# A third slot of tokens from the counts of the first eight groups, and work of the first words and the first group moved to VectorE

## The chip, the cores and the metric

The kernel runs on one core of one Trainium2 chip. The metric is device time in microseconds (us): the median of three runs before the change is 834.08 us, from 831.96 to 835.83.

## The reference

Three layers follow one another on 4 x 576 = 2304 tokens of 512 features:

```python
# attention by random features, 4 x 8 heads, 576 tokens, 64 dims, 128 features
h = q_s @ omega.T - sum(q_s**2)/2;  q_p = exp(h - max(h)) / sqrt(128)   # k_p alike
num = q_p @ (k_p.T @ v);  den = q_p . sum(k_p) + 1e-6
x = num / den
# dense feed-forward net, 512 -> 2048 -> 512
h = x @ w_in;  g = h * clip(h + 3, 0, 6) / 6;  x = g @ w_out
# mixture of 8 experts, each token goes to the one with the largest logit
logits = x @ w_gate + modality_bias[modality_id]
e = argmax(logits);  gate = softmax(logits)[e]
out[token] = gate * (relu(x @ w1[e]) @ w2[e])      # 512 -> 1024 -> 512
```

All is float32. The inputs give very uneven experts: two of the eight take 1161 and 1143 of the 2304 tokens, the others none.

## The kernel before

**Stages.** The tokens are cut into nine groups of G = 256. First the keys and values of all heads are summed up (`k_unit`). Then each group of queries goes through `q_unit` (exponentials, denominators, division, product with the summed keys and values), one unit for each pair of heads, and gives the group's rows x. Each group then runs 16 steps of the dense net; a step is one block of 128 hidden features, with a first product h (12 matmuls) and a second product y (6 matmuls). Each float32 operand is split in a high and a low part of a type that TensorE multiplies at full rate (`split`, L398), and a product is the sum of three; the low part of a step's activations is called gl, the high part gh. Group 0 works with whole float32 weights instead.

**Words.** The dense weights come as pairs of 32-bit words (the low and the high word of a wider number). `convert` (L509) makes a float32 from each pair: ScalarE takes the sign and the exponent's lead from a half word, VectorE ors the sign in, ScalarE scales the high word, and VectorE shifts and ors the rest. The first NW0 = 8 tiles of words are converted while group 0's queries are worked on; group 0's division is done head by head, on whichever of VectorE, ScalarE and GpSimd the order's cost model finds free.

**Routing.** When a group's y is done, `route` (L876) gives each token its expert, its position in a list sorted by expert, and scatters token number and gate to the table `order` in memory (DMAs on GpSimd's queue, 18 in all).

**Slots.** The expert layer works in slots of 256 tokens of one expert, numbered in the order in which they are worked on. A slot has eight steps of the same two products. Ten slots are laid out statically: the first NE from the counts of the first eight groups, by `first_slots` (L1196), which takes NE times the largest remaining count; the rest by `slot_table` (L1227) from the counts of all nine groups. The last static slot runs only its first 128 rows statically; further slots would run under a condition, and with these inputs there are none. The last group's scatter waits until the tokens of the first NE slots were loaded (the gate in `route` on `st["toks"]`), since those slots read `order` without it.

For each slot `slot_fetch` (L1125) loads the slot's token numbers from `order` (tile `tok`, on SP's queue), clips them to row numbers (`src`, on VectorE), and gathers the rows of the dense net's output (`xr<-yrows,src`, two DMAs of 128 rows on GpSimd's queue). `slot_rows` (L1146) transposes them on TensorE (eight matmuls with the identity, in the banks kp and kv) and splits them. `slot_weights` (L1091) loads each slot's 16 weight tiles (`wraw`) and splits them, on ScalarE and VectorE (`w<-wraw`). `slot_out` (L1175) scales y by the gate and scatters it to the output.

**Order.** Nothing of this is written down in a fixed order. The class `Issue` keeps all streams as tasks; its `run` (L255) asks a cost model which task could start first on which engine, takes by priority among those close together, and so writes each engine's instruction list, once, when the program is built. On the chip each engine works its list strictly in order. `t_fetch` (L1163) and `t_rows` (L1168), the streams of fetches and transposes, have the priority TOKENS (L32). A fetch may be issued once the slot before the last has its rows, and a slot's transposes once `x_free` (L1381) holds, that is when all first products of the slot before the last have been issued.

Of the kernel before, what the change touches and what calls it, by code (L numbers as in the profile page):

```python
# [18 lines left out]
P = 128  # L19
# [15 lines left out]
def f32(ap):  # L35
    return ap.bitcast(F32)
# [265 lines left out]
def favor_ffn_top1_moe_kernel(  # L302
# [28 lines left out]
    NT = N // P  # L331
    NO = E * N + G
    PAD = 1 << 20
    NE = 2
    NS_MIN = NG + 1 - NE
    NS_MAX = (N - G - (N - 2 * G) // E + E * (G - 1)) // G
    NKV = 6
    NW = 2 * KF
    NB = 4
# [128 lines left out]
    def conv():  # L468
# [40 lines left out]
        def convert(j):  # L509
            c, which = j // 2, j % 2  # L510
            yield Gate(cond=lambda: j in staged)
            t = yield from place(c, which)
            w = staged.pop(j)
            lo_w, hi_w = w[:, :, 0], w[:, :, 1]


            ti = t.bitcast(I32)
            half = w.rearrange("p n w -> p (n w)").bitcast(U16).rearrange("p (n w) -> p n w", w=4)
            yield from op(
                "A", "activation", out=ti, in_=half[:, :, 1], func=AF.Copy, scale=2.0 ** -13, bias=2.0 ** -14 - 0.5  # L520
            )

            yield from op(
                "V", "scalar_tensor_tensor", out=ti, in0=hi_w, scalar=-(1 << 31), in1=ti, op0=ALU.bitwise_and, op1=ALU.bitwise_or
            )
            yield from ts(f32(hi_w), f32(hi_w), 2.0 ** -112, ALU.mult, e="A")
            yield from op(
                "V", "scalar_tensor_tensor", out=ti, in0=hi_w, scalar=3, in1=ti,
                op0=ALU.logical_shift_left, op1=ALU.bitwise_or,
            )  # L530
            done.add(j)
            w_full[which, c] = t
# [271 lines left out]
    def q_unit(k, g, pr, tags):  # L804

        rr = list(runs(g * G, G))
        if g:
            yield from l_qh.take()
        qp, den = k.kp[0], k.den
        if k.two:  # L810
            yield from stack(qhl, k.qraw)
            mx = q.tile(rt, [P, 4], F32, "mx", 8)
            yield from project(qhl, P, GT, tags[0], qp, mx)
            pv = qp
        else:
            mx = None
            raw = k.qraw
            if g:
                raw, hi, lo = raw[:, 0], qhl[:, 0], qhl[:, 1]
                yield from split(hi, lo, raw)  # L820
            ps = bank(tags[0], [P, GT, 2 * M])
            yield q.gate("PE", [hi, lo] if g else [raw, om_f], [ps])
            for t in range(GT):
                c = slice(t * P, (t + 1) * P)
                if g:
                    mm3(ps[:, t], (hi[:, c], lo[:, c]), (om2[:, 0, :], om2[:, 1, :]))
                else:
                    do("PE", "matmul", out=ps[:, t], lhsT=raw[:, c], rhs=om_f, start=True, stop=True)
            pv = ps.rearrange("p t (h m) -> p (t h) m", m=M)
        if g:  # L830
            l_qh.give()
        yield from phi(pv, P, 2 * GT, qp, mx)
        if not all((b, pr) in z_t for _, _, b, _ in rr):
            yield Gate(cond=lambda: all((b, pr) in z_t for _, _, b, _ in rr))

        for t in range(GT):
            for o, n, b, s in runs(g * G + t * P, P):
                for h in range(2):
                    i = 2 * t + h
                    yield from op(  # L840
                        "V", "scalar_tensor_tensor", out=junk[o:o + n, i * M:(i + 1) * M], in0=qp[o:o + n, i, :], scalar=1.0,
                        in1=z_t[b, pr][o:o + n, h, :], op0=ALU.mult, op1=ALU.mult, accum_out=den[o:o + n, i:i + 1],
                    )
        yield from ts(den, den, 1e-6 * M, ALU.add)
        yield from op("V", "reciprocal", out=den, in_=den)
        if k.two:
            yield from tt(qp, qp, den.unsqueeze(2).to_broadcast([P, 2 * GT, M]), ALU.mult)
        else:
            for i in range(2 * GT):
                yield from ts(qp[:, i], qp[:, i], den[:, i:i + 1], ALU.mult, e=("V", "A", "P"))  # L850
        ps = bank(tags[-1], [P, 2, G])
        yield q.gate("PE", [qp], [ps])
        transposes([(ps[:, h, t * P:(t + 1) * P], qp[:, 2 * t + h, :]) for h in range(2) for t in range(GT)])
        yield from op(("A", "V"), "tensor_copy", out=k.qe, in_=ps)
        ps = bank(tags[0], [P, G])
        yield q.gate("PE", [k.qe] + [kv_t[b, pr] for _, _, b, _ in rr], [ps])
        for o, n, b, s in rr:

            for h in range(2):
                c = slice(h * D, (h + 1) * D)  # L860
                do(
                    "PE", "matmul", out=ps[c, o:o + n], lhsT=kv_t[b, pr][:, c], rhs=k.qe[:, h, o:o + n],
                    start=True, stop=True, skip_group_check=True,
                )
            q_open.remove(b * NPR + pr)
        if g and not (st["setup"] and st["n_in"] >= (g - 1) * KF):
            yield Gate(cond=lambda: st["setup"] and st["n_in"] >= (g - 1) * KF)
        xt = q.tile(ff, [P, 2, G], F32R if g else F32, f"x{pr}", 2)
        if g:
            yield from split(xt[:, 0], xt[:, 1], ps)  # L870
        else:
            yield from op(("A", "V"), "tensor_copy", out=xt[:, 0], in_=ps)
        x_t[g, pr] = xt
# [248 lines left out]
            done[0] = j + 1  # L1122
            st["split"] += 1

    def slot_fetch(mo, s):  # L1125

        yield q.gate("S", [s.o])
        at_ = q.load(s.o, E * N)
        s.tok = q.tile(mo, [P, GT, 2], I32, "tok", 6)
        yield from op("S", "dma_start", out=s.tok, in_=order[bass.ds(at_, G), :].rearrange("(t p) w -> p t w", p=P))  # L1130
        st["toks"] += 1
        src = q.tile(mo, [P, GT], I32, "src", 2)
        n = N if s.i >= NE else N - G
        yield from ts(src, s.tok[:, :, 0], n - 1, ALU.min)
        rows = []
        for t in range(GT):
            xr = q.tile(mo, [P, DM], F32, f"xr{t}", 2)
            yield from op(
                "P", "indirect_dma_start", out=xr, out_offset=None, in_=yrows[0:n, :],
                in_offset=bass.IndirectOffsetOnAxis(ap=src[:, t:t + 1], axis=0),  # L1140
                bounds_check=n - 1, oob_is_err=False,
            )
            rows.append(xr)
        s.rows = rows
# [16 lines left out]
        s.x = x  # L1161

    def t_fetch(mo, ss):  # L1163
        for i, s in enumerate(ss):
            yield Gate(cond=lambda: s.o is not None and (i < 2 or len(ss[i - 2].x) == KD))
            yield from slot_fetch(mo, s)

    def t_rows(ss, free):  # L1168
# [234 lines left out]
        q.run()  # L1403

    def rest(s):
        yield from slot_fetch(mo, s)
        yield from slot_rows(s, ("kp", "kv"))
        ys = None
# [63 lines left out]
```

## Time and profile before

| what | value |
| --- | --- |
| median of three runs | 834.08 us (831.96 to 835.83) |
| the profiled execution's own time | 834.48 us |
| its span in the trace | 832.8 us |
| mean granted TensorE clock | 0.983 of full speed |
| chain that ended last | issue 36%, TensorE 33%, DMA 15%, VectorE 8%, ScalarE 4% |

In the page's 40 slices TensorE's busy share is 9 tenths or more in all but five: the first two, the last, the one from 562 us (8 tenths) and the one from 625 us (5 tenths), where the granted clock is at 7 tenths. VectorE is the next busiest, with 8 or 9 tenths in most slices of the first half. The DMA engines are nearly idle from 140 to 560 us, and at 8 or 9 tenths in most slices from 625 to 770 us, where the experts' weights are loaded. Such a page is read stage by stage: an engine's share of the whole span says little of any one stage, and an idle stretch of the engine that is busy nearly all the time is time that some wait has cost.

### The profile page before, as it was taken

How to read it: one execution, taken by the hardware profiler on the slowest of the kernel's cores; microseconds unless marked ns; L12 is line 12 of the kernel's file. 1: busy time of each engine (PE TensorE's matmuls, PEld its weight loads, DVE VectorE, ACT ScalarE, POOL GpSimd, SP SyncE). 2: the span in 40 equal slices, each digit the busy share in tenths (PEclk: the TensorE clock that was granted, in tenths of full speed). 3: DMA queues.
4: the chain of work that ended last, by engine and by line, in shares of the span. 5: the costliest groups of instructions: out<-in, count | busy, mean ns of one | idle time of the engine just before them, and what ended most of it. 6: DMA issues, size and time to landing. Idle time of an engine off the chain costs nothing.

```text
span 832.8 us, 16519 instructions
## 1 busy us (share of the span) xinstructions
PE 791.0 (95%) x5395; PEld 675.0 (81%) x5395; DVE 630.8 (76%) x2135; ACT 487.1 (58%) x1245; POOL 99.7 (12%) x114
## 2 busy tenths in 40 slices
PE   7799999999999999999999999998995999999994
PEld 5476668888888888888888888987884898999993
DVE  3889999888888868878788785667986777777610
ACT  3998786777757556555655453335445766555411
POOL 0132342000000000110000000002013122211000
PEclk9989999999999999999999999999997999999997
DMA  7717574222113022221120010009359899877300
GB/s 182 278 52 228 168 243 132 51 54 83 51 33 81 13 53 68 32 61 47 41 64 27 1 39 1 26 15 289 94 171 293 276 289 273 270 219 207 103 13 29
DMA packets 108767, 96.88 MB, mean 116 GB/s; under 512 B 14847, under 2 KB 90111, under 8 KB 108672
## 3 DMA queue, kind: packets, MB, share of 16 engines
q1 hardware_dynamic: 104976, 85.75, 35.8%
q0 software_dynamic: 3696, 9.98, 3.5%
q8 instruction: 45, 0.74, 0.4%
q14 instruction: 50, 0.41, 0.2%
HBM read 86.10 MB, written 9.87 MB: 115 GB/s over the span
## 4 chain that ended last, share of the span: by engine, by line
issue 36%; PE 33%; DMA 15%; DVE 8%; ACT 4%; POOL 1%; SPq 1%; POOLq 0%; DVEq 0%; ACTq 0%
PE h L223 14%; PE y L223 9%; DMA wraw<-in_w_dram 5%; DMA order<-og,pi 4%; DVE w L223 4%; PE qa L223 3%; PE qb L223 3%; ACT w L223 2%; PE kv L223 2%; PE kp L223 2%; DMA xr<-yrows,src 1%; DMA kraw<-in_kT_dram 1%; SPq L223 1%; POOL order L223 1%; DMA w<-in_v_dram 1%
## 5 line engine op out<-in xcount | busy, mean ns | idle before, releaser
L223 PE MATMUL h<-x,w 128*128 128x256 f32 x2616 | 367.6, 290 | 2.1 <-DVE gl L223 0.9
L223 PEld LDWEIGHTS h<-x,w 128*128 128x128 f32 x2616 | 343.0, 191 | 22.5 <-issue 3.8
L223 PE MATMUL y<-w,gh 128*128 128x512 f32 x640 | 205.2, 402 | 0.0
L223 PE MATMUL y<-w,gl 128*128 128x512 f32 x320 | 126.0, 394 | 0.0
L223 PEld LDWEIGHTS y<-w,gh 128*128 128x128 f32 x640 | 110.2, 190 | 18.2 <-issue 3.0
L223 DVE TENSOR_TENSOR w<-wraw,w 128x512 fp32r<-128x512 f32 x160 | 106.3, 687 | 20.3 <-ACT w L223 16.4
L223 ACT ACTIVATE w<-wraw 128x512 fp32r<-128x512 f32 x152 | 91.2, 627 | 29.1 <-DMA wraw<-in_w_dram 25.7
L223 ACT ACTIVATE r<-h,three 128x256 f32<-128x256 f32 x144 | 68.1, 473 | 62.5 <-PE h L223 52.4
L223 DVE SCALAR_TENSOR_TENSOR junk<-st,words 128x512 bf16<-128x512 f32 x144 | 98.8, 686 | 1.2
L223 ACT ACTIVATE gh<-r 128x256 fp32r<-128x256 f32 x126 | 52.5, 417 | 80.3 <-PE y L223 75.1
L223 DVE SCALAR_TENSOR_TENSOR r<-r,h 128x256 f32<-128x256 f32 x144 | 60.3, 419 | 28.2 <-ACT r L223 24.8
L223 DVE TENSOR_TENSOR gl<-r,gh 128x256 fp32r<-128x256 f32 x128 | 54.3, 424 | 34.4 <-ACT gh L223 22.0
L223 PEld LDWEIGHTS y<-w,gl 128*128 128x128 f32 x320 | 60.5, 189 | 14.3 <-DVE gl L223 0.3
L223 POOL DMA_INDIRECT order<-og,pi x18 | 19.1, 1064 | 406.9 <-DVE pi L223 261.4
L223 ACT ACTIVATE gh<-h 128x256 fp32r<-128x256 f32 x72 | 27.4, 380 | 60.1 <-PE qb L223 22.4
L223 DVE SCALAR_TENSOR_TENSOR gl<-h,gh 128x256 fp32r<-128x256 f32 x72 | 30.4, 422 | 31.9 <-ACT gh L223 29.1
L223 ACT ACTIVATE kp<-kp,mx 112x128 f32<-112x128 f32 (+1 forms) x120 | 38.8, 387 | 1.2 <-DVE mx L223 1.0
L223 POOL DMA_INDIRECT out_dram<-st,tok x19 | 19.8, 1040 | 162.5 <-ACT gh L223 77.7
L223 DVE SCALAR_TENSOR_TENSOR junk<-qp,zb 128x128 bf16<-128x128 f32 (+1 forms) x144 | 37.4, 286 | 1.4 <-ACT qp L223 0.2
L223 ACT ACTIVATE qp<-qp,mx 128x128 f32<-128x128 f32 x104 | 36.2, 393 | 0.0
L223 DVE SCALAR_TENSOR_TENSOR w<-words,w 128x512 int32<-128x512 int32 x44 | 31.7, 748 | 0.0
L223 PE MATMUL kp<-om,khl 128*112 128x256 f32 (+1 forms) x140 | 29.4, 307 | 1.5 <-DVE khl L223 1.0
(270 smaller groups left out, 1069.4 us busy)
## 6 DMA issues: line engine op xcount, KB each, us to landing
wraw<-in_w_dram SPq DMA_DIRECT2D x160, 256.0 KB
words<-in_w_in_dram SPq DMA_DIRECT2D x12, 512.0 KB
words<-in_w_out_dram SPq DMA_DIRECT2D x12, 512.0 KB
qraw<-in_qT_dram SPq DMA_DIRECT2D x36, 128.0 KB
yrows<-st SPq DMA_DIRECT2D x18, 256.0 KB
kraw<-in_kT_dram SPq DMA_DIRECT2D x40, 112.0 KB
vraw<-in_v_dram SPq DMA_DIRECT2D x24, 112.0 KB
w<-in_w_in_dram SPq DMA_DIRECT2D x4, 512.0 KB
```

Source lines behind the costliest of these rows:

```text
L223: return getattr(self.eng[e], m)(**kw)
```

## The change

Three edits, in four places of the code:

1. `NE` goes from 2 to 3, so `first_slots` picks three slots; `NS_MIN` falls from 8 to 7 with it, the static slots stay ten, and `NS_MAX`, the bound on slots of the table, falls from 15 to 14. The load of a slot's tokens is taken out of `slot_fetch` into `slot_tokens`, and `t_fetch` loads the tokens of all three first slots before the first slot's `src`. `src` gets three buffers instead of two.
2. For the first eight tiles of words, `convert` uses one scaling on ScalarE, one scaling on VectorE (which carries the sign) and two shift-and-or operations on VectorE, instead of the half-word operation and the scaling on ScalarE with two such operations on VectorE.
3. Group 0's division is one VectorE operation for a unit, not four small ones on three engines.

```diff
--- before.py
+++ after.py
@@ -331,9 +331,13 @@
     NT = N // P
     NO = E * N + G
     PAD = 1 << 20
-    NE = 2
+    NE = 3
     NS_MIN = NG + 1 - NE
-    NS_MAX = (N - G - (N - 2 * G) // E + E * (G - 1)) // G
+
+    taken_min = G
+    for _ in range(NE - 1):
+        taken_min += min(G, -(-(N - G - taken_min) // E))
+    NS_MAX = (N - taken_min + E * (G - 1)) // G
     NKV = 6
     NW = 2 * KF
     NB = 4
@@ -512,6 +516,18 @@
             t = yield from place(c, which)
             w = staged.pop(j)
             lo_w, hi_w = w[:, :, 0], w[:, :, 1]
+            if j < NW0:
+
+                ti = t.bitcast(I32)
+                yield from ts(f32(hi_w), f32(hi_w), 2.0 ** -112, ALU.mult, e="A")
+                yield from ts(t, f32(hi_w), 2.0 ** -126, ALU.mult)
+                for w_, n, f in ((lo_w, 29, ALU.logical_shift_right), (hi_w, 3, ALU.logical_shift_left)):
+                    yield from op(
+                        "V", "scalar_tensor_tensor", out=ti, in0=w_, scalar=n, in1=ti, op0=f, op1=ALU.bitwise_or
+                    )
+                done.add(j)
+                w_full[which, c] = t
+                return
 
 
             ti = t.bitcast(I32)
@@ -843,7 +859,7 @@
                     )
         yield from ts(den, den, 1e-6 * M, ALU.add)
         yield from op("V", "reciprocal", out=den, in_=den)
-        if k.two:
+        if k.two or not g:
             yield from tt(qp, qp, den.unsqueeze(2).to_broadcast([P, 2 * GT, M]), ALU.mult)
         else:
             for i in range(2 * GT):
@@ -1122,14 +1138,16 @@
             done[0] = j + 1
             st["split"] += 1
 
-    def slot_fetch(mo, s):
-
+    def slot_tokens(mo, s):
         yield q.gate("S", [s.o])
         at_ = q.load(s.o, E * N)
         s.tok = q.tile(mo, [P, GT, 2], I32, "tok", 6)
         yield from op("S", "dma_start", out=s.tok, in_=order[bass.ds(at_, G), :].rearrange("(t p) w -> p t w", p=P))
         st["toks"] += 1
-        src = q.tile(mo, [P, GT], I32, "src", 2)
+
+    def slot_fetch(mo, s):
+
+        src = q.tile(mo, [P, GT], I32, "src", NE)
         n = N if s.i >= NE else N - G
         yield from ts(src, s.tok[:, :, 0], n - 1, ALU.min)
         rows = []
@@ -1161,8 +1179,13 @@
         s.x = x
 
     def t_fetch(mo, ss):
+        for s in ss[:NE]:
+            yield Gate(cond=lambda: s.o is not None)
+            yield from slot_tokens(mo, s)
         for i, s in enumerate(ss):
             yield Gate(cond=lambda: s.o is not None and (i < 2 or len(ss[i - 2].x) == KD))
+            if i >= NE:
+                yield from slot_tokens(mo, s)
             yield from slot_fetch(mo, s)
 
     def t_rows(ss, free):
@@ -1403,6 +1426,7 @@
         q.run()
 
     def rest(s):
+        yield from slot_tokens(mo, s)
         yield from slot_fetch(mo, s)
         yield from slot_rows(s, ("kp", "kv"))
         ys = None
```

What the order makes of the first edit shows best on three engines' lists, behind the count of the first eight groups.

VectorE before: the small operations of `first_slots` (c, h, mx, eo, taken), slot 0's `src`, and the first split of an expert's weights (`w<-wraw,w`):

```order
L223 TENSOR_TENSOR h_7063<-h_7063 128x8
L223 TENSOR_TENSOR gl<-r,gh 128x256
L223 TENSOR_REDUCE mx_7062<-h_7063 128x1
L223 CAST eo<-mx_7062 128x1
L223 TENSOR_SCALAR mx_7062<-mx_7062 128x1
L223 TENSOR_SCALAR h_7063<-h_7063,mx_7062 128x8
L223 TENSOR_SCALAR src<-tok 128x2
L223 TENSOR_TENSOR taken<-taken,h_7063 128x8
L223 TENSOR_TENSOR c_7045<-c_7045,h_7063 128x8
L223 TENSOR_TENSOR w<-wraw,w 128x512
L223 SCALAR_TENSOR_TENSOR r<-r,h_7150 128x256
```

VectorE with the change, the same place; the second `src` is slot 1's:

```order
L223 TENSOR_SCALAR mx_7059<-mx_7059 128x1
L223 TENSOR_TENSOR gl<-r,gh 128x256
L223 TENSOR_SCALAR h_7060<-h_7060,mx_7059 128x8
L223 TENSOR_TENSOR w<-wraw,w 128x512
L223 TENSOR_TENSOR taken<-taken,h_7060 128x8
L223 TENSOR_TENSOR c_7043<-c_7043,h_7060 128x8
L223 TENSOR_TENSOR w<-wraw,w 128x512
L223 TENSOR_SCALAR src<-tok 128x2
L223 TENSOR_TENSOR w<-wraw,w 128x512
L223 TENSOR_SCALAR st<-y_6761 128x512
L223 TENSOR_TENSOR w<-wraw,w 128x512
L223 TENSOR_SCALAR src<-tok 128x2
```

Slot 0's `src` stood three rows ahead of the first weight split; it now stands behind the group's last difference (`gl<-r,gh`) and in the middle of the weight splits, six of which come ahead of it from there and the rows before.

TensorE before: slot 0's second four transposes (bank kv, rows `xr_7185` and `xr_7193`) end, its first two steps' products h follow, and slot 1's transposes (`xr_7315`, `xr_7321`) come behind them:

```order
L223 MATMUL kv<-ident,xr_7185 128x128
L223 MATMUL kv<-ident,xr_7193 128x128
L223 MATMUL h_7367<-x_7302,w 128x256 x3
L223 MATMUL h_7367<-x_7317,w 128x256 x3
L223 MATMUL h_7367<-x_7349,w 128x256 x3
L223 MATMUL h_7367<-x_7358,w 128x256 x3
L223 MATMUL h_7392<-x_7302,w 128x256 x3
L223 MATMUL h_7392<-x_7317,w 128x256 x3
L223 MATMUL h_7392<-x_7349,w 128x256 x3
L223 MATMUL h_7392<-x_7358,w 128x256 x3
L223 MATMUL kp<-ident,xr_7315 128x128
L223 MATMUL kp<-ident,xr_7321 128x128
```

TensorE with the change: slot 1's transposes (`xr_7329`, `xr_7339`) stand ahead of slot 0's first product:

```order
L223 MATMUL kv<-ident,xr_7306 128x128
L223 MATMUL kv<-ident,xr_7314 128x128
L223 MATMUL kv<-ident,xr_7306 128x128
L223 MATMUL kv<-ident,xr_7314 128x128
L223 MATMUL kp<-ident,xr_7329 128x128
L223 MATMUL kp<-ident,xr_7339 128x128
L223 MATMUL kp<-ident,xr_7329 128x128
L223 MATMUL kp<-ident,xr_7339 128x128
L223 MATMUL h_7417<-x_7356,w 128x256 x3
L223 MATMUL h_7417<-x_7378,w 128x256 x3
```

The first product of slot 0 so stands behind the gathers of both slots.

GpSimd's queue before, from the last scatters of the first eight groups (`order` x16) on; the gathers of slots 0 and 1, the output of slot 0 (`out_dram`) and the last group's scatter, and slot 2's gathers (`xr_8038`, `xr_8048`):

```order
L223 DMA order<-og,pi 18688x2 x16
L223 DMA xr_7185<-yrows,src 128x512
L223 DMA xr_7193<-yrows,src 128x512
L223 DMA xr_7315<-yrows,src 128x512
L223 DMA xr_7321<-yrows,src 128x512
L223 DMA out_dram<-st,tok 2304x512 x2
L223 DMA order<-og,pi 18688x2 x2
L223 DMA out_dram<-st,tok 2304x512
L223 DMA xr_8038<-yrows,src 128x512
L223 DMA xr_8048<-yrows,src 128x512
```

GpSimd's queue with the change; `xr_7414` and `xr_7477` are slot 2's rows:

```order
L223 DMA order<-og,pi 18688x2 x16
L223 DMA xr_7306<-yrows,src 128x512
L223 DMA xr_7314<-yrows,src 128x512
L223 DMA xr_7329<-yrows,src 128x512
L223 DMA xr_7339<-yrows,src 128x512
L223 DMA xr_7414<-yrows,src 128x512
L223 DMA xr_7477<-yrows,src 128x512
L223 DMA out_dram<-st,tok 2304x512 x2
L223 DMA order<-og,pi 18688x2 x2
L223 DMA out_dram<-st,tok 2304x512 x2
L223 DMA xr_8279<-yrows,src 128x512
L223 DMA xr_8286<-yrows,src 128x512
```

Slot 2's gathers moved from behind the last group's scatter to ahead of slot 0's output.

## Rows read from the trace of the kernel before

**Rows 1.** The page's first part: engine, busy us, share of the span, instructions.

```profile
PE 791.0 (95%) x5395; PEld 675.0 (81%) x5395; DVE 630.8 (76%) x2135; ACT 487.1 (58%) x1245; POOL 99.7 (12%) x114
```

**Rows 2.** TensorE's waits, 560 to 645 us: us, times, longest.

```profile
PE kp L223 <- DMA xr<-yrows,src: 10.9, 3, 8.0
```

**Rows 3.** Timeline, slot 1's end to slot 2: start, us, engine, operation [wait].

```profile
624.13 0.40 PE L223 MATMUL y<-w,gl 128*128 128x512 f32 x1
...
626.80 0.17 DVE L223 TENSOR_SCALAR src<-tok 128x2 int32<-128x2 int32 x1
...
627.75 1.38 POOL L223 DMA_INDIRECT xr<-yrows,src  x1 [1.20 <-issue]
...
629.43 1.01 POOL L223 DMA_INDIRECT xr<-yrows,src  x1 [0.31 <-issue]
...
632.50 0.45 PE L223 MATMUL kp<-ident,xr 128*128 128x128 f32 x1 [7.97 <-DMA xr<-yrows,src]
...
635.29 0.90 PE L223 MATMUL kp<-ident,xr 128*128 128x128 f32 x3 [2.34 <-DMA xr<-yrows,src]
...
636.70 6.29 PE L223 MATMUL h<-x,w 128*128 128x256 f32 x36
...
642.83 0.63 PE L223 MATMUL qa<-w,gh 128*128 128x512 f32 x2
```

**Rows 4.** Busy time by stretch, slot 2's start: engines, clock, DMA share.

```profile
632.50:637.00 4.50, 2.15 (x9) 1.81 (x9) 1.00 (x3) 0.38 (x1) 2.03 (x2) 0.50 0.99 301
```

**Rows 5.** Timeline from the count of eight groups to slot 0's first products.

```profile
554.06 0.18 PE L223 MATMUL kv<-acc,ones 128*128 128x8 bf16 x1
...
563.61 1.05 POOL L223 DMA_INDIRECT xr<-yrows,src  x1 [7.80 <-DMA wraw<-in_w_dram]
...
564.97 1.01 POOL L223 DMA_INDIRECT xr<-yrows,src  x1 [0.31 <-issue]
...
571.03 0.55 PE L223 MATMUL kp<-ident,xr 128*128 128x128 f32 x3 [0.56 <-DMA xr<-yrows,src]
...
573.23 1.53 POOL L223 DMA_INDIRECT xr<-yrows,src  x1 [7.25 <-DVE src L223]
...
575.76 0.60 PE L223 MATMUL kv<-ident,xr 128*128 128x128 f32 x4
...
576.11 1.10 PE L223 MATMUL h<-x,w 128*128 128x256 f32 x7
...
577.63 2.58 PE L223 MATMUL h<-x,w 128*128 128x256 f32 x15 [0.42 <-DVE x L223]
```

**Rows 6.** The chain that ended last: one first and one second product.

```profile
582.27 1.43 PE h L223 x12
...
715.60 1.39 PE y L223 x6
```

**Rows 7.** Costliest groups, VectorE: busy us, mean ns, idle before.

```profile
L223 DVE TENSOR_TENSOR w<-wraw,w 128x512 fp32r<-128x512 f32 x160 | 106.3, 687 | 20.3 <-ACT w L223 16.4 <-issue 0.5
...
L223 DVE TENSOR_TENSOR gl<-r,gh 128x256 fp32r<-128x256 f32 x128 | 54.3, 424 | 34.4 <-ACT gh L223 22.0 <-PE kp L223 7.7 <-PE qa L223 1.8
...
L223 DVE SCALAR_TENSOR_TENSOR w<-words,w 128x512 int32<-128x512 int32 x44 | 31.7, 748 | 0.0
...
L223 DVE TENSOR_TENSOR qp<-qp,den 128x512 f32<-128x512 f32 x26 | 17.9, 687 | 0.2
...
L223 DVE CAST w<-wraw 128x512 fp32r<-128x512 f32 x8 | 3.4, 426 | 1.6 <-DMA wraw<-in_w_dram 1.6
```

**Rows 8.** Timeline: slot 1's first product, the last group's positions.

```profile
599.98 1.59 PE L223 MATMUL h<-x,w 128*128 128x256 f32 x12
...
606.88 0.16 DVE L223 CAST pi<-pf 128x2 int32<-128x2 f32 x1
```

**Rows 9.** Busy time by stretch, two early ones, columns as in group 4.

```profile
21.00:47.00 26.00, 19.87 (x162) 13.24 (x158) 20.21 (x71) 24.21 (x77) 6.15 (x9) 0.87 0.68 239
...
60.00:140.00 80.00, 78.17 (x474) 54.49 (x473) 76.28 (x177) 66.16 (x167) 28.49 (x26) 1.00 0.64 197
```

## Prediction

> **What bounds the kernel now.** I read the page first, then TensorE's waits, then the timeline where the long waits stand. The page gives TensorE 791.0 us of a span of 832.8 us [rows 1], so nearly every idle TensorE microsecond counts and other engines' work mostly does not. The waits between 560 and 645 us have one large entry: 10.9 us in three waits for gathered token rows, the longest 8.0 us [rows 2]. The timeline shows its place: the last product of slot 1 starts at 624.13 and ends at 624.53, the first matmul of slot 2 starts at 636.70 [rows 3]. The gathers of slot 2 are issued at 627.75 and 629.43 and the second has landed by 635.29. They are late because slot 2 is the first slot of the table, and the table needs the counts of all nine groups. The granted clock is 0.50 in 632.50 to 637.00, the lower level (1.2 GHz), after eight idle microseconds [rows 4].
>
> The same chain (tokens, row numbers, gather, transposes) stands before slot 0. I count there from c = 554.06, the matmul that counts the first eight groups' tokens: first gather at c+9.55, just behind its row numbers (src), second at c+10.9, landed at c+17.0, first matmul of slot 0 at c+22.05 [rows 5]. One step's first product takes 1.43 us at full clock, its second 1.39 [rows 6].
>
> **The sum, part by part.** It is made against the profiled execution, 834.48 us, span 832.8; the runs' median is 834.08, so the sum's difference is put on 834.08. Less than 0.5% of that (4.2 us) can hardly be told from no change.
>
> *Term 1, the wait before slot 2 goes: -13.3.* Slot 2's tokens are now known with eight groups' counts; slots 0 and 1 cover the table. From 624.53 to 636.70 are 12.17 us, in which the eight transposes (0.35 for four at full clock, 576.11 less 575.76, so 0.70) stay: -11.47. The 36 matmuls behind took 6.13 us (642.83 less 636.70) where three steps at 1.43 take 4.29: -1.84 more [rows 3, 5, 6]. Slot 2's weights come from the same counts, their expert known with slot 0's. On GpSimd's queue its gathers now stand ahead of slot 0's scatters of the output; they wait for slot 0's row buffers, which its transposes free long before those scatters.
>
> *Term 2, a longer wait before slot 0: +8.0 (5 to 11).* The loads of all three slots' tokens now come ahead of the first src, each waiting on SP for its numbers from VectorE, with weight loads queued behind; those are needed later, so SP costs nothing. But VectorE's order moves: src of slot 0 stood three rows ahead of the first weight split of that stretch; now it stands behind the last difference (gl) of the group and behind six splits. Engines run in order, so src waits for all of it. That gl needs the buffer of two steps before, free when the second y behind the last h ends: 4 x 1.43 + 5 x 1.39 = c+12.7. A copy and a difference, 0.42 each, with hand-overs make c+13.9 (estimate), two splits of 0.69 and small operations c+15.8 [rows 6, 7]. Weights that land late push it: I take c+16.6, and c+18 as the far end, since DMA was full before slot 2, at a share of 0.99 [rows 4]. From src to the first gather is 0.95, from one gather to the next 1.36 to 1.68, from a gather to its landing 4.75 to 6.06 [rows 3, 5]. TensorE's order now wants slot 1's gathers as well before slot 0's first matmul, so four gathers count: 16.6 + 0.95 + 3 x 1.45 + 5.3 + 0.35 for four transposes = c+27.5. Against c+22.05 that is +5.45. The count now stands one step nearer to the group's end (four h behind it, not five): +1.43. Four transposes are done earlier: -0.35. A wait of 0.42 behind slot 0's first matmuls goes, and a lowered clock as in term 1 comes: -0.42 + 1.84. Sum 7.95. Low end: src at c+15.8, gathers 1.36 apart landing in 4.75, no lowered clock, 4.5. High end: c+18, 1.68, 6.06: 10.9.
>
> Beside that stands a page of the Trainium skill. The trace has a gather issue of 1.53 us at 573.23, while a weight split ran, beside 1.01 at 564.97 [rows 5]. The Trainium skill (SBUF — State Buffer, section "SBUF: two separate sides") says GpSimd and VectorE take turns, for whole instructions, on one pair of ports when VectorE runs a two-port form or reads two SBUF inputs. By that rule all four gather issues would be stretched, and term 2 would be about 2 us more.
>
> *Term 3, the table comes due before slot 3: +1.0 (0 to 4).* Before, the positions of the last group were ready at 606.88, slot 2's src at 626.80 and its rows at 635.29: 28.4 us [rows 3, 8]. In the new order the positions stand in slot 1's fourth step. Slot 0 takes 23.87 us (599.98 less 576.11), slot 1 24.55 (624.53 less 599.98), three and a half steps 9.9: the positions come 33.8 us after slot 0's first matmul. Slot 3's transposes stand behind slot 2's sixth h: 23.87 + 24.55 + 6 x 1.43 + 5 x 1.39 = 63.95. That leaves 30.2. But sixteen weight splits now stand among the table's small operations on VectorE, 16 x 0.69 = 11 us, where it partly waited before: I put 4 us on the chain, so 32.4 against 30.2 plus the 1.84 of the low clock.
>
> *Term 4, the first words and the division: +1.2 (-1 to +6.2).* VectorE gets eight multiplications of 128x512 and four divisions of 128x512 at 0.69; GpSimd loses five small ones, ScalarE eight sign conversions and ten small divisions. The multiplication has no row. Its ends are 0.43 (a one-source cast, 128x512, from SBUF) and 0.75 (the two-source operation on the same strided words) [rows 7]; I take 0.43, as it has one source. VectorE gets 8 x 0.43 + 4 x 0.69 = 6.2. In 21 to 47 us it is busy 20.21 of 26, ScalarE 24.21 [rows 9]: 5.8 of room, and the fuller engine is relieved. From 60 to 140 VectorE is busy 76.28 of 80, TensorE 78.17; what does not fit earlier shows there. I take 0.4 of spill and 0.8 because three more words' operations stand before the reductions of group 0's queries. If nothing covers it, all 6.2 show; if ScalarE's relief is what counts, a microsecond is won.
>
> The Trainium skill (VectorE: DVE Perf Modes, section "What auto-detection actually checks") gives one-source operations in SBUF the doubled rate with no word on strides. By it the eight cost 3.4 us; by the row with two sources they would cost 6.0 and the term would be 3.8.
>
> Sum: -13.3 + 8.0 + 1.0 + 1.2 = -3.1, so **831.0 us**.
>
> **Rivals.** *A, the gathers are in time (0.17).* Term 2 at its low end, nothing in terms 3 and 4: -13.3 + 4.5 gives 825.3. For it: fewer transfers compete ahead of the first gather. Against: src cannot pass the last gl. *B, the wait moves one slot on (0.11), the slow side.* The place is VectorE between the count of the last group and the table. If the splits there wait for weights, table, tokens and gathers slip together. It decides for slower once term 3 passes 8.3, that is a chain of some 40 us from positions to landed rows instead of 28.4; at 10 it gives 831.0 + 9 = 840.0. For it: DMA ran full there. Against: the weights of slot 2 were asked for long before. *C, VectorE is the bound of the first phase (0.15).* Term 4 at 6.2: 836.0, no difference to be told. For it: 95% busy in 60 to 140. Against: its new work stands mostly before 50. *D, slot 2 waits all the same (0.05)*, for weights or because the third slot is no early one: without term 1, terms 2 and 4 give 843.3. Against: its transposes stand in slot 0's last step.
>
> **Chances.** My own case has 0.52, centred on 831.0 and spread by 3 or 4 us, so 0.23 of it lies under 829.9 and 0.29 between. With A faster is 0.40; with C and a little of B same is 0.44; B and D make slower 0.16. The range 825.0 to 839.0 takes in A, C and the unknown ends of terms 2 to 4 and leaves out most of B and D.
>
> **What would show it.** Right: no long wait before slot 2; a wait of 6 to 9 us before slot 0 ended by gathered rows, with a lowered clock behind it; src of slot 0 some 16 us after the count; less than 3 us before slot 3; TensorE's idle time from 21 to 47 us, 6.1 now, within 1.5 us of that. Wrong: the wait before slot 0 under 3 us (too high), over 8 us before slot 3, or TensorE idle over 5 us more in 60 to 140 us (both too low).

## The result, and the profile after

The changed kernel takes 844.09 us (median of 8 runs, 839.72 to 847.92) where the kernel before takes 835.05 (8 runs): a ratio of 1.0117, 95% interval 1.0096 to 1.0139. It is **slower by about 9 us**; forecast were 831.0 us, in a range of 825 to 839. The profiled execution took 844.36 us, its span is 842.5 us, 9.7 longer than before.

The page's first part for the changed kernel, against [rows 1]:

```profile
PE 793.3 (94%) x5399; PEld 676.1 (80%) x5399; DVE 630.7 (75%) x2135; ACT 488.5 (58%) x1236; POOL 95.7 (11%) x113
```

TensorE's busy time grew by 2.3 us, so 7.4 us of the 9.7 are idle time. TensorE's waits from 555 to 690 us (in total, times, longest), where the kernel before has the one large entry of [rows 2], one of 1.7 us and three under 0.5:

```profile
PE kp L223 <- issue: 7.3, 1, 7.3
PE kp L223 <- DMA xr<-yrows,src: 4.9, 2, 2.7
PE y L223 <- ACT gh L223: 1.8, 3, 1.0
PE kp L223 <- DVE x L223: 1.2, 1, 1.2
```

The wait before slot 2 is gone, as the change says. In its place stand 10.7 us before slot 0 (7.27 to the first gathered tile, which the profile puts down to "issue", that is to nothing that it shows; 2.18 to the second; 1.24 for the bank) and 2.69 before slot 3. The waits for activations (ACT gh) are short: 0.96 in the last group, 0.45 and 0.40 in slot 1. To see where the 9.7 us arise, the timeline of ScalarE gives four places that both programs have in the same order: the 137th of 144 activations of the dense net (the last group's ninth step), and the fifth step of slots 1, 2 and 3. Before:

```profile
547.07 0.47 ACT L223 ACTIVATE r<-h,three 128x256 f32<-128x256 f32 x1 [1.30 <-PE h L223]
...
613.11 0.38 ACT L223 ACTIVATE gh<-h 128x256 fp32r<-128x256 f32 x1
...
651.15 0.37 ACT L223 ACTIVATE gh<-h 128x256 fp32r<-128x256 f32 x1
...
675.09 0.36 ACT L223 ACTIVATE gh<-h 128x256 fp32r<-128x256 f32 x1
```

After:

```profile
549.46 0.48 ACT L223 ACTIVATE r<-h,three 128x256 f32<-128x256 f32 x1 [1.24 <-PE h L223]
...
629.51 0.37 ACT L223 ACTIVATE gh<-h 128x256 fp32r<-128x256 f32 x1
...
655.70 0.37 ACT L223 ACTIVATE gh<-h 128x256 fp32r<-128x256 f32 x1
...
683.87 0.37 ACT L223 ACTIVATE gh<-h 128x256 fp32r<-128x256 f32 x1
```

The differences are +2.39, +16.40, +4.55 and +8.78 us. Slot 0's first product moved from 576.11 to 590.03, by 13.92. Term 2 of the forecast has a part behind slot 0's first product, the lowered clock less a wait of 0.42 (+1.42), and is split there. So the stretches cost, in order:

| stretch | forecast | in the trace |
| --- | --- | --- |
| up to the last group's ninth step (term 4) | +1.2 | +2.4 |
| to slot 0's first product (term 2 up to there) | +6.5 | 13.92 - 2.39 = +11.5 |
| to slot 1's fifth step (the rest of term 2) | +1.4 | 16.40 - 13.92 = +2.5 |
| to slot 2's fifth step (term 1) | -13.3 | 4.55 - 16.40 = -11.9 |
| to slot 3's fifth step and the end (term 3) | +1.0 | 9.7 - 4.55 = +5.1 |

Every term missed on the same side. These are differences of two single executions.

**Slot 0.** The timeline from the count on:

```profile
559.33 0.18 PE L223 MATMUL kv<-acc,ones 128*128 128x8 bf16 x1
...
575.65 0.38 SPq L223 DMA_DIRECT2D tok<-order  x1
...
576.76 0.16 DVE L223 TENSOR_SCALAR src<-tok 128x2 int32<-128x2 int32 x1
...
577.91 1.05 POOL L223 DMA_INDIRECT xr<-yrows,src  x1 [16.59 <-ACT w L223]
...
578.81 2.62 DVE L223 TENSOR_TENSOR w<-wraw,w 128x512 fp32r<-128x512 f32 x4
579.26 1.11 POOL L223 DMA_INDIRECT xr<-yrows,src  x1 [0.31 <-issue]
...
580.68 1.00 POOL L223 DMA_INDIRECT xr<-yrows,src  x1 [0.30 <-issue]
...
581.99 1.52 POOL L223 DMA_INDIRECT xr<-yrows,src  x1 [0.30 <-issue]
...
583.58 0.45 PE L223 MATMUL kp<-ident,xr 128*128 128x128 f32 x1 [7.27 <-issue]
...
586.21 0.90 PE L223 MATMUL kp<-ident,xr 128*128 128x128 f32 x3 [2.18 <-DMA xr<-yrows,src]
...
589.21 1.16 PE L223 MATMUL kp<-ident,xr 128*128 128x128 f32 x4 [1.24 <-DVE x L223]
...
590.03 0.56 PE L223 MATMUL h<-x,w 128*128 128x256 f32 x1
```

Counted from c = 559.33, src stands at c+17.4 and the first product at c+30.7 [rows 5 had c+22.05]. The third token load, 575.65, stands behind the third pick, and `t_fetch` lays src behind that load. The fourth gather is issued at c+22.7. The view by tile gives the time from issue to landing of these four gathers, and the start of the second of slot 1's transposes:

```profile
DMA to landing us min/median/max: 5.6/6.9/7.4
...
L223 PE MATMUL kp<-ident,xr x1: 475/475/475, 589.5 to 589.5; 128*128 128x128 f32 x1
```

The fourth took the longest, 7.4 us, and so landed at 589.4, just ahead of the transpose that reads it. The 1.24 us for the bank (slot 1's first transpose waits until slot 0's rows are split) end at 589.21 and so cost next to nothing of their own: the last landing sets the pace.

**Slot 3.** VectorE from the last group's positions (pi) to the end of the table (tab) and src of slot 3:

```profile
624.14 0.33 DVE L223 CAST pi<-pf 128x2 int32<-128x2 f32 x1
...
631.99 0.69 DVE L223 TENSOR_TENSOR w<-wraw,w 128x512 fp32r<-128x512 f32 x1 [1.25 <-ACT w L223]
...
637.75 0.69 DVE L223 TENSOR_TENSOR w<-wraw,w 128x512 fp32r<-128x512 f32 x1 [1.23 <-ACT w L223]
...
639.78 0.69 DVE L223 TENSOR_TENSOR w<-wraw,w 128x512 fp32r<-128x512 f32 x1 [0.94 <-ACT w L223]
...
647.29 0.17 DVE L223 TENSOR_SCALAR tab<-js 128x14 int32<-128x14 f32 x1
...
653.60 0.16 DVE L223 TENSOR_SCALAR src<-tok 128x2 int32<-128x2 int32 x1
```

Its end in the kernel before, and the wait before slot 3 with the change:

```profile
620.70 0.17 DVE L223 TENSOR_SCALAR tab<-js 128x15 int32<-128x15 f32 x1
```

```profile
662.59 0.55 PE L223 MATMUL kp<-ident,xr 128*128 128x128 f32 x3 [2.69 <-DMA xr<-yrows,src]
```

The table took 23.15 us, where the same two instructions stood 13.8 us apart before (606.88 [rows 8] and 620.70). Between its small operations stand splits that wait for their weights, and the table, behind them on the same engine, waits with them.

**The first words.** In the costliest groups of the stretch from 21 to 60 us the added operations are short (eight multiplications, four divisions; busy us, mean ns):

```profile
L223 DVE TENSOR_SCALAR w<-w 128x512 f32<-128x512 f32 x8 | 3.4, 429 | 0.0
...
L223 DVE TENSOR_TENSOR w<-w 128x512 f32<-128x512 f32 x4 | 2.7, 688 | 0.0
```

TensorE's wait for the division of group 0 and group 0's first product (h<-x,w), before and after:

```profile
37.61 0.91 PE L223 MATMUL kp<-ident,w 128*128 128x128 f32 x4 [3.07 <-ACT w L223]
...
47.22 1.02 PE L223 MATMUL h<-x,w 128*128 128x256 f32 x4
```

```profile
42.28 1.05 PE L223 MATMUL kp<-ident,w 128*128 128x128 f32 x4 [4.79 <-DVE w L223]
...
49.64 0.70 PE L223 MATMUL h<-x,w 128*128 128x256 f32 x2 [0.48 <-ACT x L223]
```

Group 0's first product is 2.4 us later, as much as the +2.4 at the last group's ninth step. But two executions cannot tell whose this is. In the traces of the experiments below it stands between 45.49 and 48.30 us in the old order (the kernel before and runs 1, 4, 7, 8, 9, 11 and 13), and between 47.34 and 49.64 with both edits (this one and runs 2, 3, 12): by the means some 1.7 us later, with a spread as large.

### The profile page after: what moved, and what is told of

It reads as the page before. It is cut to its first block, busy times and chain, and to the rows that moved or that the text cites. A ratio compares the mean times of both kernels' runs of the same rounds, so it can differ in the third digit from the quotient of the medians.

```text
span 842.5 us, 16406 instructions
## 1 busy us (share of the span) xinstructions
PE 793.3 (94%) x5399; PEld 676.1 (80%) x5399; DVE 630.7 (75%) x2135; ACT 488.5 (58%) x1236; POOL 95.7 (11%) x113
## 5 line engine op out<-in xcount | busy, mean ns | idle before, releaser
L223 DVE TENSOR_TENSOR w<-wraw,w 128x512 fp32r<-128x512 f32 x160 | 108.3, 688 | 30.1 <-ACT w L223 26.8
L223 ACT ACTIVATE w<-wraw 128x512 fp32r<-128x512 f32 x156 | 95.7, 629 | 45.5 <-DMA wraw<-in_w_dram 37.2
L223 DVE SCALAR_TENSOR_TENSOR r<-r,h 128x256 f32<-128x256 f32 x144 | 60.4, 419 | 19.2 <-ACT r L223 15.7
L223 ACT ACTIVATE qp<-qp,mx 128x128 f32<-128x128 f32 x96 | 34.0, 394 | 0.0
```

Of the source, the lines that this page charges most:

```text
L223: return getattr(self.eng[e], m)(**kw)
```

## The experiments

Ratios are to the kernel before on the same chip, with 95% intervals; a difference of medians of two runs from different chips is rougher than the ratios. In the expectations A, B and C are theories of the whole loss, D to G of the VectorE edits.

**The parts by themselves.** Run 1 leaves the two VectorE edits out, run 2 makes them alone:

> The change without its two edits on VectorE (first words' signs, first group's division as before). Theory A, read from the two traces: of the 9.7 us lost, the third slot with the loads of all tokens ahead of the first src costs 7.3 and the VectorE edits 2.4. So this run is about 842 us, 7 over the kernel before: TensorE waits some 10 us before slot 0 and hardly at all before slot 2. Theory B, the VectorE edits cost the most, and the order behind them merely differs: 836 us or less. Theory C, the loads of the experts' weights set the pace of the stretch whatever waits for what: 842 too, with the lost time in waits for weights.

> The kernel before with the two VectorE edits alone (two early slots, as before). Theory A: 2 to 3 us slower, 837.5 us, all of it ahead of the first product of group 0; the waits before slots 0 and 2 as in the kernel before (2.3 and 10 us). Theory B: 842 us or more. Theory C says nothing here beyond A.

Measured: 838.51 us (ratio 1.0039, 1.0009 to 1.0070) for the third slot alone, 844.15 (1.0136, 1.0077 to 1.0196) for the VectorE edits alone. Theory A, read from one trace, is wrong with both its figures (842 and 837.5). Theory B, that the VectorE edits cost the most, holds for run 2; its 836 or less for run 1 does not, since the third slot does not gain. Run 1's profiled execution (841.44 us, 2.9 above its median) is 0.5 us late at the last group's ninth step and then splits much as the changed kernel's: +9.1, +3.1, -11.1 and +5.3 in the table's next four rows, with the same 7.3 us wait before slot 0. So these stretches come with the third slot, though their sum, 6.8 with the 0.5, is more than the 2.5 that the medians show.

**Tokens in turn.** Runs 3 and 4 load slot 2's tokens behind the src and gathers of slots 0 and 1, with and without the VectorE edits:

```diff
-        for s in ss[:NE]:
-            yield Gate(cond=lambda: s.o is not None)
-            yield from slot_tokens(mo, s)
         for i, s in enumerate(ss):
...
-            if i >= NE:
+            if i < 2 or i >= NE:
                 yield from slot_tokens(mo, s)
             yield from slot_fetch(mo, s)
+            if i == 1:
+                for z in ss[2:NE]:
+                    yield Gate(cond=lambda: z.o is not None)
+                    yield from slot_tokens(mo, z)
```

> The whole change, but the tokens of slot 2 are loaded behind the src and gathers of slots 0 and 1, so that src of slot 0 stands where it stood in the kernel before. Theory A, src of slot 0 is late because it stands behind the third pick of a slot and the splits among it: the wait before slot 0 falls from some 10 us to 2 to 4, the one before slot 2 stays gone, and a wait before slot 3 of 3 to 6 stays: 834 us, 10 under the change, the same as before. Theory C, the weights' loads set the pace: what is won before slot 0 is lost again before slot 3, 842 to 844 us.

> As the run before, without the two VectorE edits. Theory A: 2 to 3 us less than that run, 831.5 us, faster than the kernel before by 3 to 4. Theory B: under 828. Theory C: 839 to 842.

Measured: 839.72 us (1.0039, 1.0003 to 1.0074) with them, 834.98 (0.9998, 0.9976 to 1.0021) without. None of the theories gave either figure. The loads' place cost some 4 us in both pairs by the medians (844.09 to 839.72, 838.51 to 834.98; by the ratios 6.5 and 3.4), less than the 10 that the wait before slot 0 suggested. The traces show a new wait in its place: in the fourth run TensorE waits 3.52 us in slot 0 for a weight split (the timeline, PE):

```profile
593.65 0.50 PE L223 MATMUL qa<-w,gh 128*128 128x512 f32 x1 [3.52 <-DVE w L223]
```

**The third pick and the table.** Run 7 starts from run 4 and holds the third pick back until src of slot 1 is recorded; run 8 also holds the splits back while the table is made:

```diff
+            if i >= 2:
+                yield Gate(cond=lambda: st["src"] >= 2)
             mx, me, mo_ = m[:, 0:1], m[:, 1:2], m[:, 2:3]
...
-            yield Gate(cond=lambda: j in raws and free(j))
+            yield Gate(cond=lambda: j in raws and free(j) and (st["routed"] < NG or st["tab"]))
```

> The third slot alone, with tokens in turn (834.98 us) and the third pick held back until src of slot 1 is recorded, so that the third pick's thirteen small operations and the third token load stand behind the gathers of slots 0 and 1. If src of slot 1 behind the third pick is what made slot 1 late there (its weights and rows 5 us later than before), this wins 3 to 5 us: 830 to 832. If it was the weights' loads that waited on SP behind the third token load, it wins as much; the issue times of the loads then tell the two apart. If the wait only moves to slot 3, whose table comes later still, 834 to 836.

> As the run before, and no weight split is recorded between the last group's scatters and the end of the table. In the changed kernel the table took 23.2 us from the last positions to its end, beside 13.8 before, with splits that wait for weights between its small operations. If these are what makes slot 3 wait: the table within 12 us of the positions, no wait before slot 3, and 2 to 4 us under the run before, 827 to 829. If the splits that are held back make slot 1 or 2 wait for weights instead: no gain, 831 to 834.

Measured: 830.66 us (0.9951, 0.9924 to 0.9977) and **823.94 us** (0.9878, 0.9858 to 0.9897), both as expected or better. The second beats both kernels. For run 7 I had two reasons beforehand, slot 1's src or the weight loads behind the third token load. Slot 1's src stands at 571.16 us in run 4 and 570.97 in run 7, so it is not that one. SP's queue in run 4, and in run 7:

```profile
566.86 4.76 SPq L223 DMA_DIRECT2D wraw<-in_w_dram  x5
572.42 0.38 SPq L223 DMA_DIRECT2D tok<-order  x1
574.26 2.68 SPq L223 DMA_DIRECT2D wraw<-in_w_dram  x2
```

```profile
565.51 11.55 SPq L223 DMA_DIRECT2D wraw<-in_w_dram  x9
```

From 565 to 578 us these are nine weight loads instead of seven, and the wait for a weight split in slot 0 falls from 3.52 to 1.36. So it was the loads, as far as one trace of each can show.

VectorE in run 7, and in run 8:

```profile
609.65 0.16 DVE L223 CAST pi<-pf 128x2 int32<-128x2 f32 x1
...
639.14 0.16 DVE L223 TENSOR_SCALAR tab<-js 128x14 int32<-128x14 f32 x1
```

```profile
607.80 0.19 DVE L223 CAST pi<-pf 128x2 int32<-128x2 f32 x1
...
620.27 0.17 DVE L223 TENSOR_SCALAR tab<-js 128x14 int32<-128x14 f32 x1
```

The table falls from 29.5 to 12.5 us. TensorE's waits for gathered rows (555 to 690 us of run 8), 10.9 in [rows 2], are now:

```profile
PE kp L223 <- issue: 1.6, 1, 1.6
PE kp L223 <- DMA xr<-yrows,src: 1.6, 2, 1.1
```

The kernel before has a wait put down to issue there too, of 1.7.

Run 11 takes the table first with two early slots only:

> The kernel before (two early slots) with no weight split recorded between the last group's scatters and the end of the table. If the third slot is what made the version with the table first fast (823.94), this wins little: the table stands 13.8 us behind the positions here, and 12.5 there, so the wait before slot 2 falls by 1 to 2 us of 10: 832 to 835. If the table's place alone did it: 824 to 827.

Measured: 836.61 us (1.0017, 0.9995 to 1.0039), no difference: a little above the expected band, and far from the other theory's. The table's place gains nothing without the third slot; the third slot gains 4 us without the table's place (run 7) and 11 with it (run 8).

**Which VectorE edit?** Runs 5 and 6 make one each on the kernel before:

> The kernel before with the first words' signs on VectorE alone. Both VectorE edits together cost 8 us (844.15 beside 835.98), of which the trace shows 2.5 before the first product of group 0 and 4.8 at the end of the dense net. Theory D, the eight added operations of 0.43 us and the operations that they push back fill VectorE ahead of group 0's first product: this run carries most of it, 840 to 843 us. Theory E, the wide division is what costs, because the first transposes of group 0 now wait for one long operation behind all four denominators: this run is at 836 to 838.

> The kernel before with the first group's division as one VectorE operation alone. Theory D: 836 to 838 us, the first product of group 0 within 1 us of the kernel before. Theory E: 840 to 843, with the first product of group 0 some 2 us later.

Measured: 842.13 us for the signs (1.0106, 1.0064 to 1.0148) and 848.59 for the division (1.0157, 1.0130 to 1.0184). Each by itself costs 7 or 13 us, and both together 8: no sum of operations does that, so D and E both fall. The program's lists show what the two share: behind the first group, operations of later keys and queries change engine, form and place, in stretches that the edits do not touch. With both edits, for example, TensorE has 72 matmuls each of qa and qb from qhl instead of 70.

**Operations or order?** Run 9 adds VectorE work that the planner is not told of, run 10 tells the planner of work that isn't there:

```diff
+            if j < NW0:
+                nc.vector.tensor_scalar(out=junk, in0=t, scalar1=1.0, scalar2=None, op0=ALU.mult)
             done.add(j)
```

```diff
+            if j < NW0:
+                q.clk["V"] += 0.35
             done.add(j)
```

> The kernel before, with eight more VectorE multiplications of 128x512, one behind the last operation on each of the first eight tiles of words, that write to a scratch tile; the planner is not told of them, so every other instruction stands where it stood. This is the VectorE time that the signs' edit adds (8 x 0.43 = 3.4 us), without the order that followed from it. Theory F, the price of the VectorE edits is the operations themselves: 838 to 842 us, as the signs alone (842.13). Theory G, the price is the order that the planner makes of everything behind them: 835 to 837.5, at most 2.5 over the kernel before and all of that ahead of the first product of group 0.

> The kernel before without any added work: the planner's own clock of VectorE is put forward by 0.35 us, its price of such a multiplication, at the same eight places, so that it lays out everything behind them as if they were there. Theory F: 834 to 836.5 us, as the kernel before. Theory G: 839 to 845, with the loss in the dense part and spread over several short waits for keys' and queries' operands (khl, qhl), as in the runs with one edit.

Measured: 836.29 us (1.0004, 0.9976 to 1.0032) for the work, 846.16 (1.0117, 1.0078 to 1.0157) for the order. The added multiplications took 464 ns each in the trace, 3.7 us in all, and vanish. Run 13 goes on to the edit itself: its own operations for the signs, while the planner prices the old ones (`op_as` plans with the operands it is given and emits another instruction):

```diff
+                yield from q.op_as("A", "activation", scale_hi, out=ti, in_=half[:, :, 1])
+                yield from q.op_as("V", "scalar_tensor_tensor", sign, out=ti, in0=hi_w, in1=ti)
...
```

> The kernel before with the signs' edit made in it (ScalarE's half-word operation gone, a VectorE multiplication and the other shift added, the first eight tiles of words), while the planner goes on pricing the old operations, so that all else stands as in the kernel before. The same edit with the order that the planner made of it was at 842.13 us. Theory F, the operations' own price: 839 to 843. Theory G, the order's price: 834 to 837, like the kernel before.

Measured: 836.25 us (1.0005, 0.9984 to 1.0025). The signs' edit in the old order costs nothing that can be told, and 7 us in the order that the planner makes of it ("order" takes in the engines and forms that the planner chooses). The division was not run in the old order, so that its 13 us are the order's alone is not shown; in its trace group 0's first product stands at 47.68, within the spread of the old order. Runs 14 and 15 shift the planner's clock as run 10 does, by +0.10 and -0.20 us:

> The kernel before with no instruction added or changed by hand; the planner's clock of VectorE goes forward by 0.10 us, not 0.35, at the eight places. If the price of an order comes with a fuller VectorE in the planner's eyes, a third of the shift costs a third or less: 836 to 840 us. If any shift ends in another order whose time is a matter of luck, the result is anywhere from 833 to 846 and says nothing of the shift's size.

> The same with the clock put back by 0.20 us at the eight places. If a fuller VectorE in the planner's eyes is what costs, this is no slower than the kernel before: 832 to 836.5 us. If any shift from the order found before costs by luck: anywhere from 833 to 846.

Measured: 850.87 us (1.0201, 1.0154 to 1.0248) and 848.44 (1.0146, 1.0111 to 1.0182). Neither size nor sign of the shift says anything; the results lie even above the band that I gave to chance. Six orders of the dense part other than the old one were run on two early slots (runs 2, 5, 6, 10, 14, 15): 842 to 851 us, each slower than the old one by 7 us or more. Much of it shows in the dense part. TensorE's busy time from 60 to 556 us (the first number behind the stretch's length of 496.00), in the kernel before, in run 13 (old order), in the changed kernel, in run 10 and in run 14:

```profile
60.00:556.00 496.00, 492.20 (x3447) 416.06 (x3447) 410.10 (x1587) 306.98 (x821) 45.69 (x42) 1.00 0.24 68
```

```profile
60.00:556.00 496.00, 492.15 (x3439) 414.96 (x3438) 409.95 (x1584) 309.02 (x824) 44.61 (x41) 1.00 0.25 68
```

```profile
60.00:556.00 496.00, 489.39 (x3448) 413.28 (x3443) 405.02 (x1566) 309.02 (x823) 44.49 (x46) 1.00 0.23 66
```

```profile
60.00:556.00 496.00, 487.63 (x3404) 409.93 (x3403) 407.51 (x1553) 306.54 (x816) 46.20 (x48) 1.00 0.25 67
```

```profile
60.00:556.00 496.00, 480.35 (x3341) 403.52 (x3340) 400.17 (x1541) 304.55 (x811) 38.47 (x41) 0.99 0.24 68
```

Idle time goes from 3.8 us in the old order to 6.6, 8.4 and 15.7 in the others. From group 0's first activation in the dense net to the ninth step of the last group the eight traces in the old order take 496.8 to 498.5 us, runs 10, 15 and 14 take 503.4, 511.1 and 514.2: 5 of run 10's 10 us arise here, and all of run 14's. With both edits it is 497.5 in the changed kernel and 499.1, 499.4 and 500.4 in runs 12, 3 and 2. So their order costs at most 2.5 us here and some 1.7 ahead of group 0's first product; the rest of its price lies behind the ninth step.

**All together.** Run 12 is run 8 with the VectorE edits:

> The whole change, VectorE edits included, with tokens in turn, the third pick late and the table ahead of the splits. Theory G, the VectorE edits cost through the order of the dense part, which this version shares with the changed kernel up to the count: 3 to 8 us over the same version without them (823.94), 827 to 832. If the edits' price sat behind the count and went with the waits there: 824 to 826.

Measured: 835.33 us (1.0006, 0.9979 to 1.0033), 11.4 over run 8 (10.7 by the ratios) and more than any theory gave: the edits, with their order, take back the whole gain. Its trace has a wait of 4.2 us for a weight split in slot 0 where run 8 has 1.4, a part of the price behind the count.

## Why the prediction was wrong

**Term 4, the step that failed most.** I priced the signs and the division by the operations that they add (6.2 us of VectorE, nearly all covered) and took 1.2 us. The operations' durations were right: 429 ns for each multiplication against 0.43 taken, 688 for each division against 0.69; and the signs' show no loss in the old order. What I put at nothing is that the planner lays out all later work anew whenever one price in it changes. The two edits with the order that follows cost 8.2 us by themselves (844.15 less 835.98), and 5.6 on top of the third slot (844.09 less 838.51; 6.5 by the ratios). Runs 10, 14 and 15 show that an order alone can cost that much; only for the division is its own share open. Rival C gave the wrong reason, for VectorE is no fuller in 60 to 140 us (75.28 of 80, before 76.28), and only a part of the loss lies in its stretch.

**Terms 1 to 3.** Their sum was -4.3 us; the third slot alone came out at +2.5 by the medians (838.51 less 835.98). The terms one by one can only be read from traces, and the two that have the third slot up front (the changed kernel and run 1) agree on them within some 2.5 us.
- Term 1: -11.9 where I had -13.3; the mechanism held.
- Term 2: +11.5 up to slot 0's first product, where I had 6.5 (8.0 with the clock behind it, 11 as the far end). The count came 2.88 us nearer to the group's end (5.27 less 2.39), a whole step of a first and a second product; I had charged the first product alone, 1.43. src at c+17.4 lay within my c+16.6 to c+18, and the gathers followed one another as forecast. But the fourth landed 7.4 us behind its issue, where I had 5.3, and 6.06 as the far end, from three gathers of the kernel before. That is 2.1 of the 3.5 us by which the chain from the count overran its forecast; why it landed so late is open. "SP costs nothing" was also too quick: runs 4 and 7 show weight loads held up behind the third token load, and late splits from it.
- Behind slot 0's first product: 2.5 us where term 2 had 1.42. The lowered clock came as forecast, at 2.40 instead of 1.84: the 24 matmuls of h took 5.26 us, to 595.29, where two steps at 1.43 take 2.86. The granted clock was 0.55, near the lower of its two levels (1.2 GHz), after 13.7 us in which TensorE was busy for 3.00 (columns as in [rows 4]):

```profile
576.30:590.00 13.70, 3.00 (x13) 2.25 (x13) 8.60 (x18) 6.58 (x14) 4.68 (x4) 0.57 0.90 271
590.00:596.00 6.00, 6.00 (x32) 5.96 (x30) 4.77 (x16) 1.94 (x6) 2.46 (x2) 0.55 0.83 252
```

- Term 3: +5.1 where I had +1.0 and 4 as the far end (the prediction's own figures, 32.4 against 30.2 and 1.84, give 0.4; the rest of the 1.0 has no source). The positions came as forecast, 34.1 us after slot 0's first product (33.8). The chain behind them took 38.45 us to slot 3's rows at 662.59, and I had 32.4: I put 4 us on the table for the splits among its operations, and they cost 9.3 (23.15 less 13.8). The wait that came of it was 2.69 us, because the slots before ran late too. Run 8 takes exactly these splits away and wins 6.7 us over run 7, whose table took 29.5.

**The rivals.** B named the place, VectorE between the last positions and the table, and a chain of some 40 us; that mechanism came (38.45 us), at half the price, and I gave it 0.11. The chances had no case in which several small losses add up with an order that is simply worse, though the lists of both programs showed other engines and forms far from the edits.

**The signs.** Nearly all that I named as signs of being right came: no long wait before slot 2, a wait before slot 0 ended by gathered rows (9.45 us without the bank, for 6 to 9) with a lowered clock behind it, src at c+17.4, under 3 us before slot 3, idle time from 21 to 47 us within 1.5 of 6.1 (7.5). None of the signs of being wrong came; TensorE is idle 3.0 of 80 us from 60 to 140, 1.2 more than before. The total was still 13 us off, for no sign watched the sum of small losses.

**The rule on ports.** The prediction's second figure for term 2, 2 us more, had all four gather issues stretched. The rows above have 1.05, 1.11, 1.00 and 1.52 us, and VectorE ran four splits with two SBUF inputs back to back from 578.81 to 581.43, beside the second and third. So issues of about a microsecond pass beside such splits, and only the last looks stretched; the forecast without that rule was nearer. The Trainium skill (SBUF — State Buffer, section "SBUF: two separate sides") counts two SBUF inputs only against a GpSimd operation that reads SBUF, and reports a probe in which `tensor_tensor`, the splits' operation, did not stall DMA. The trace agrees for the second and third gather; the prediction left that limit out.

## What to carry to other kernels

Where a planner writes the order, an edit's price is that of its operations plus that of another order, and the two can be measured apart: make the edit and keep the planner blind to it, or shift the planner's clock and leave the work alone. Compare a change only with the spread that such empty shifts give, here 10 to 15 us on the slow side of an order that was better than six others. And when a wait is moved off one chain, look at the next chain that is due on the same in-order engine: small operations that decide something for other engines should not stand among large ones that wait for data.

## What the runs showed of the hardware

The signs' added multiplications cost nothing that can be told (ratio 0.9984 to 1.0025 in run 13) on a VectorE that is busy 20.21 of 26 us around them [rows 9], while the order in which the engines get their work is worth up to 15 us in 835 (run 14), with no instruction changed by hand. Four gathers of 128 rows, issued within 4.1 us at a DMA share of 0.90, landed 5.6 to 7.4 us after their issue; in the kernel before the first use came 4.75 to 6.06 behind the issue [rows 3, 5], and in run 8 (560 to 640 us) gathers landed after 3.5 to 6.7.
